# The local attention's result: transposed by VectorE on its way to DRAM, or by TensorE on its way back

## The chip, the core and the metric

One core of a Trainium2 chip. Its engines are TensorE (PE, with PEld for its weight loads), VectorE (DVE), ScalarE (ACT), GpSimd (POOL) and SyncE (SP), which issues nearly all the DMAs. The metric is the device time of one execution in microseconds, the median of several runs.

## The reference

Two attentions over the same input x (2048 positions, 448 features, 16 heads of 28), mixed by a gate. All is float32.

```python
x = A_x
g = sigmoid((x * gate_w).sum(-1, keepdims=True))
# A, local: position s looks at s, s-2, ..., s-14 (eight places)
logits = einsum("bhsd,bhswd->bhsw", q, k[s - 2w]) * 28 ** -0.5   # masked where s - 2w < 0
a = (softmax(logits) applied to v[s - 2w]).reshape(B, S, D) @ A_wo
# B, full: softmax(q k^T * 28 ** -0.5) v over all 2048 positions
b = (...).reshape(B, S, D) @ B_wo
return g * a + (1 - g) * b
```

## The kernel before, in words

Each float32 operand of a matmul is split into two parts, a rounded one (`hi`) and the rest (`lo`), and a product is three matmuls (hi hi, hi lo, lo hi; `TERMS`). The program is written for five engines in an order of its own; nothing is reordered afterwards, and each engine works through its list in order.

**First stage** (to about 260 us): the projections of x to q, k, v of both attentions.

**Attention, 256 steps.** A unit `u` (0 to 15) is four heads and 512 queries; a step is one block of 128 keys of a unit (`kt`, sixteen in a unit), so step 121 is unit 7, block 9. In a step PE makes the scores of the four heads (function `scores`, L1024), ACT takes two exponentials (L1027, each of 128x1024, into one of the tiles `P`), and PE multiplies the step before's probabilities with V (`do_av`, L978). In the trace a step begins with its first exponential. The maxima that the softmax of B needs are made ahead: in steps 0 to 234 PE also makes up to three plain score tiles (L144) and DVE reduces them (L148, a tile of 128x512 and then a pair); the pair's bank serves the next step's scores.

**Local attention beside it.** Attention A runs on POOL and DVE during those steps, in eight chunks of two heads. A chunk `c` is: eight products q k (POOL, `a_score`, L613) with their sums (DVE, `a_reduce`, L623), a softmax (`a_softmax`), and eight products with v and seven adds into the tile `oat` (POOL, `a_av`, L663 and L668). Rows of `oat` are positions (128 partitions x 16), columns 2 heads of 28. A planner writes the order: `item(engine, key, name, cost, needs, f)` puts an instruction on an engine's list, `needs` are names with a lag in steps, and `issue` takes at each step, in order of key, what is due. It books the costs of POOL and DVE against about 2.25 us a step; POOL may be booked up to 4.2 us behind, DVE up to 0.7. Four steps after a chunk's last add one DMA puts `oat` into `oa_scr` in DRAM, by positions.

**Output projection.** When the planner's lists are empty (`a_done`, step 217) the output weights are loaded and split (`raw_wo`, `split_wo`). From step 236 on, `op_some` puts items of a queue (`op_queue`) behind each step, seven a step: for each of sixteen blocks `j` of 128 positions, the local result is loaded (`op_load_a`), transposed by PE (`op_t`, four transposes, L795), split by ACT and DVE (`op_split`, L803 to L806) and multiplied (`op_mm`, L817) with the weights, together with B's result, which is feature-major already (`op_load_b`, from `on_hi` and `on_lo`). Blocks 12 to 15 and the rest of 8 to 11 come after the last step. Working tiles come from a ring of eight buffers of 128x512 (`mtile`).

B's result of a unit goes through a chain of its own, one unit later (`fin_copy` to `fin_store`): the sum of the exponentials to DRAM and back, its inverse spread, a product on POOL, a split, a store.

## Time and profile before

| | |
|---|---|
| median of 3 runs | 918.61 us (916.68 to 918.8) |
| the profiled execution | 918.6 us, its span 916.7 us |
| granted TensorE clock | 0.997 |
| busy | PE 904.7, DVE 731.4, ACT 652.1, POOL 620.9 us |
| 300 to 700 us | POOL busy 43.7 to 49.6 of every 50 us, DVE 47.2 to 49.2 |
| 800 to 880 us | POOL busy 0 to 1.3 of every 20 us, DVE 1.5 to 2.2, PE 20.0 |

The profile is of one execution. A group's line tells the code line, the engine, the operation, the tiles (out<-in), shapes and count, then the busy time in us, the mean duration of one in ns, and the idle time of the engine ahead of it with what ended it. A line of the timeline begins with its start and length in us. PE's matmuls are pipelined: the next one starts before the last one's end, so that the distance of starts tells what one costs, not its duration.

### The profile page before, as it was taken

The page shows a single profiled execution, that of the slowest core. Times are in us where ns is not written, and L with a number is a line of the kernel's source. Part 1 is how long each engine was busy: PE and PEld are TensorE (multiplying, and loading weights), DVE is VectorE, ACT ScalarE, POOL GpSimd, SP SyncE. Part 2 cuts the span into 40 slices and gives each one's busy share as a digit, 9 for nine tenths or more (in the row PEclk, how much of TensorE's full clock was granted, in tenths as well). Part 3 has the DMA queues.
Part 4 walks back from the last instruction along what each step waited for, and adds up shares of the span by engine and source line. Part 5 has one row for each costly group of instructions (what it writes and reads, how often), then busy time and mean ns, then how long its engine had stood idle before and what let it go on. Part 6 is the DMA issues. An engine that isn't in the chain of part 4 may idle for free.

```text
span 916.7 us, 20680 instructions
## 1 busy us (share of the span) xinstructions
PE 904.7 (99%) x8396; PEld 539.3 (59%) x8396; DVE 731.4 (80%) x977; ACT 652.1 (71%) x802; POOL 620.9 (68%) x485
## 2 busy tenths in 40 slices
PE   9899999999999999999999999999999999999998
PEld 7688999999954444444444444443444444466667
DVE  6388999999979999999999999999999888400012
ACT  6356434343378898888888898988989889854551
POOL 2289856564469799999999999999994952300100
PEclk9999999999999999999999999999999999999999
DMA  9867603444372341335135232530412123553422
GB/s 268 275 203 220 177 11 83 132 122 120 103 249 70 97 126 44 86 112 127 44 96 153 86 102 55 144 79 23 115 42 53 34 66 102 145 162 112 131 90 93
DMA packets 101118, 104.29 MB, mean 114 GB/s; under 512 B 61652, under 2 KB 71252, under 8 KB 100240
## 3 DMA queue, kind: packets, MB, share of 16 engines
q1 hardware_dynamic: 100880, 102.72, 39.5%
q8 instruction: 65, 1.06, 0.5%
q10 hardware_dynamic: 144, 0.26, 0.1%
q14 instruction: 29, 0.24, 0.1%
HBM read 61.99 MB, written 40.48 MB: 112 GB/s over the span
## 4 chain that ended last, share of the span: by engine, by line
PE 80%; POOL 11%; DMA 3%; SPq 2%; ACT 2%; issue 1%; DVE 0%; POOLq 0%; ACTq 0%; DVEq 0%
PE T L1024 22%; PE av L978 20%; PE r L298 15%; PE T L817 8%; PE r L293 7%; PE r L144 4%; POOL prod L613 3%; POOL oat L668 3%; PE T L144 3%; POOL prod L663 2%; SPq L101 2%; ACT P L1027 1%; PE T L795 1%; DMA KL<-qk_lo 1%; DMA V<-in_xT 1%
## 5 line engine op out<-in xcount | busy, mean ns | idle before, releaser
L1027 ACT ACTIVATE P<-T 128x1024 f32<-128x1024 f32 x512 | 497.4, 1025 | 81.0 <-PE T L1024 79.6
L148 DVE TENSOR_REDUCE MX<-T 128x1 f32<-128x512 f32 x470 | 441.3, 954 | 33.6 <-PE T L144 19.6
L978 PE MATMUL av<-P,V 128*32 128x512 f32 x2048 | 272.7, 605 | 0.0
L1024 PEld LDWEIGHTS T<-QH,KH 30*128 30x128 f32 x1024 | 90.8, 181 | 222.4 <-ACT P L1027 199.9
L144 PE MATMUL T<-KH,QP 28*128 28x512 f32 x704 | 219.6, 454 | 0.1
L162 DVE TENSOR_REDUCE MX<-r 128x2 f32<-128x1024 f32 x160 | 192.5, 1221 | 28.3 <-PE r L144 23.6
L1024 PE MATMUL T<-QH,KH 30*128 30x512 f32 x1024 | 211.2, 489 | 3.0 <-ACT P L1027 2.0
L1024 PE MATMUL T<-QH,KL 28*128 28x512 f32 x1024 | 185.7, 395 | 0.0
L1024 PE MATMUL T<-QL,KH 28*128 28x512 f32 x1024 | 183.5, 392 | 0.0
L613 POOL TENSOR_TENSOR prod<-qt,kt 128x896 f32<-128x896 f32 x64 | 135.2, 2117 | 1.4 <-DMA kt<-a_scr 1.4
L362 ACT ACTIVATE raw<-r 128x896 f32<-128x896 f32 (+1 forms) x64 | 58.9, 921 | 96.7 <-PE r L298 96.7
L668 POOL TENSOR_TENSOR oat<-oat,prod 128x896 f32<-128x896 f32 x56 | 118.3, 2113 | 2.4
L144 PE MATMUL r<-KH,QP 64*128 64x512 f32 x320 | 98.9, 393 | 3.4 <-DMA KH<-qk_hi 3.4
L144 PEld LDWEIGHTS T<-KH,QP 28*128 28x128 f32 x704 | 86.0, 181 | 27.1 <-ACT P L1027 20.3
L663 POOL TENSOR_TENSOR prod<-vt,L 128x896 f32<-128x896 f32 x56 | 95.6, 1708 | 0.5
L363 POOL TENSOR_TENSOR ast<-raw 128x448 f32<-128x448 f32 x48 | 55.5, 1156 | 57.8 <-ACT raw L362 49.4
L1024 PEld LDWEIGHTS T<-QL,KH 28*128 28x128 f32 x1024 | 93.3, 184 | 0.0
L1024 PEld LDWEIGHTS T<-QH,KL 28*128 28x128 f32 x1024 | 91.8, 183 | 0.9
L298 PE MATMUL r<-wh,xh 64*128 64x448 f32 (+1 forms) x512 | 87.8, 363 | 0.0
L978 PEld LDWEIGHTS av<-P,V 128*32 128x32 f32 x2048 | 40.3, 108 | 77.2 <-issue 72.2
L805 DVE TENSOR_TENSOR oalo<-T,oah 128x384 fp32r<-128x384 f32 x16 | 8.9, 557 | 90.8 <-ACT onhi L804 87.7
L298 PE MATMUL r<-wh,xl 64*128 64x448 f32 (+1 forms) x384 | 70.9, 363 | 0.0
(110 smaller groups left out, 1157.0 us busy)
## 6 DMA issues: line engine op xcount, KB each, us to landing
a_scr<-ast SPq DMA_DIRECT2D x24, 448.0 KB
qk_hi<-qkh SPq DMA_DIRECT2D x24, 256.0 KB
qk_lo<-qkh SPq DMA_DIRECT2D x24, 256.0 KB
rbc<-rs SPq DMA_DIRECT2D x60, 64.0 KB
QP<-qk_hi SPq DMA_DIRECT2D x64, 56.0 KB
KL<-qk_lo SPq DMA_DIRECT2D x16, 224.0 KB
QH<-qk_hi SPq DMA_DIRECT2D x64, 56.0 KB
QL<-qk_lo SPq DMA_DIRECT2D x64, 56.0 KB
```

The lines of the kernel that those rows point to most:

```text
L144: nc.tensor.matmul(bank, qhis[u][h % 2][r, 128 * qs:128 * qs + 128], KH[u // NB % 3][r, 512 * kc:512 * kc + 512], start=True, stop=True)
L148: r = nc.vector.tensor_reduce(MX[:, n % NMX:n % NMX + k], bank, axis=X, op=ALU.max)
L162: nc.vector.tensor_reduce(m, PM[k], axis=X, op=ALU.max)
L293: nc.tensor.matmul(bank, ws[c][rows, k, t[4]:t[4] + 128], x, start=first, stop=last)
L298: nc.tensor.matmul(bank[:, 0:cols], x, ws[c][rows, k, 0:cols], start=first, stop=last)
L613: nc.gpsimd.tensor_tensor(out=p, in0=qt[c], in1=kvt["k", c % 2][:, HALO - DIL * w:HALO - DIL * w + NJ, :], op=ALU.mult)
L663: nc.gpsimd.tensor_tensor(out=dst.rearrange("p j (h d) -> p j h d", d=DH), in0=kvt["v", c % 2][:, HALO - DIL * w:HALO - DIL * w + NJ, :].r ...
L668: nc.gpsimd.tensor_tensor(out=oat[c], in0=oat[c], in1=oat[c, w], op=ALU.add)
L817: writes(bank, nc.tensor.matmul(bank[:, :D], src, wo[c][:, k, :], start=(first and k == ks[0] and i == 0), stop=(last and k == ks[-1] and ...
L978: nc.tensor.matmul(av[32 * h:32 * h + 32, :], V[:, kt, 4 * g + h, :], tiles_[h], start=(kt == 0), stop=(kt == NJ - 1), skip_group_check=True)
L1024: nc.tensor.matmul(bank[a], (KH[g % 3], KH[g % 3], KL[g % 2])[t][r, ks], (qh, ql, qh)[t][r, :], start=(t == 0), stop=(t == 2))
L1027: e = nc.scalar.activation(p, RP[0] if a == "2" else mine, AF.Exp, scale=SCALE).ins
```

## The change

`oat` gets rows of 32 for each head (28 used, the rest zero): two tiles `oats` that alternate. After a chunk's last add DVE transposes it in 32x32 blocks, four instructions of 128x256 (`a_turn`, new line L676), and eight DMAs (`a_store`, two for each group of 32 partitions) write the blocks' rows, 32 values of 4 bytes a piece, into `oa_scr`, which is now feature-major. Both are items of the planner. The projection then loads four tiles of 512 positions for each of four blocks `b`, and DVE and POOL split them (`op_split`, into parts of the old K tiles, `spare`, that the attention no longer reads). `op_t` is gone from PE. The projection queue is served five items a step instead of seven. There are four tiles `P` instead of eight.

```diff
-    oa_scr = dram.tile([128, NJ, D], F32, name="oa_scr")
+    oa_scr = dram.tile([D, S], F32, name="oa_scr")
-    probs = [ep.tile([128, 2, 512], F32, name=f"P{i}") for i in range(8)]
+    probs = [ep.tile([128, 2, 512], F32, name=f"P{i}") for i in range(4)]
+    oats = [a1.tile([128, NJ, 2, 32], F32, name=f"oat{i}") for i in range(2)]
+    for t in oats:
+        nc.gpsimd.memset(t, 0.0)
...
-            if w == W - 1:
-                stored[0] = now[0] + 4
-                at("end", stored[0], lambda: nc.sync.dma_start(oa_scr[:, :, 56 * c:56 * c + 56], oat[c]))
+    def a_turn(c, i):
+        if i == 0:
+            oaTt[c] = a2.tile([128, NJ, 2, 32], F32, name="oatT")
+        r = slice(4 * i, 4 * i + 4)
+        nc.vector.transpose(oaTt[c][:, r].rearrange("p j h e -> p (j h e)"),
+                            oats[c % 2][:, r].rearrange("p j h e -> p (j h e)"))
+    def a_store(c, a):
+        for h in range(2):
+            f = 56 * c + DH * h
+            nc.sync.dma_start(oa_scr[f:f + DH].rearrange("f (j p) -> f j p", j=NJ)[:, :, 32 * a:32 * a + 32],
+                              oaTt[c][32 * a:32 * a + DH, :, h, :])
...
+        for i in range(4):
+            item("dve", c0 + 53 + i, ("t", c, i), 0.35, [(("a", c, W - 1, 1), 1), (("t", c, i - 1), 0)],
+                 lambda c=c, i=i: a_turn(c, i))
+            item("sp", c0 + 59 + i, ("st", c, i), 0, [(("t", c, 3), 2), (("st", c, i - 1), 1)],
+                 lambda c=c, i=i: a_store(c, i))
...
+    def op_load_a(b):
+        cs = slice(512 * b, 512 * b + 512)
+        for k in range(4):
+            raws[b, k] = mtile("oar")
+            n = 128 if k < 3 else 64
+            nc.sync.dma_start(raws[b, k][0:n, :], oa_scr[128 * k:128 * k + n, cs])
+    def op_split(b, k):
...
+        nc.vector.tensor_copy(hi, raw)
+        nc.gpsimd.tensor_tensor(out=lo, in0=raw, in1=hi.bitcast(F32), op=ALU.subtract)
-    def op_t(j):
...
-            (0, lambda: op_t(j + 1)),
-            (0, lambda: op_split(j + 1)),
...
-    at("end", OP0 + 3, lambda: (op_load_a(0), op_load_a(1)))
+    at("end", OP0 + 3, lambda: op_load_a(0))
+    for k in range(4):
+        at("dve", OP0 + 6 + k, lambda k=k: op_split(0, k))
...
-                op_some(st, 7)
+                op_some(st, 5)
```

The first place is DVE in steps 120 to 122, where chunk 3's last add has been issued to POOL in step 120. A step's rows are the two maxima (L148) and what the planner adds behind them; L623 and L626 are the same sums of the local scores. Before:

```order
L623 TENSOR_REDUCE L<-prod 128x16 x2
L148 TENSOR_REDUCE MX<-T_3283 128x1
L148 TENSOR_REDUCE MX<-T_3271 128x2
L148 TENSOR_REDUCE MX<-T_3283 128x1
L148 TENSOR_REDUCE MX<-T_3275 128x2
L623 TENSOR_REDUCE L<-prod 128x8 x2
```

And in the changed kernel:

```order
L626 TENSOR_REDUCE L<-prod 128x16 x2
L148 TENSOR_REDUCE MX<-T_3283 128x1
L148 TENSOR_REDUCE MX<-T_3271 128x2
L676 STREAM_TRANSPOSE oatT<-oat_3316 128x256
L148 TENSOR_REDUCE MX<-T_3283 128x1
L148 TENSOR_REDUCE MX<-T_3275 128x2
L626 TENSOR_REDUCE L<-prod 128x8 x2
```

The first of the chunk's four transposes stands in the step right behind the add's, ahead of the next step's maxima.

The second place is PE in the first step with projection work, step 236. `oah` and `oalo` are the split local result, `KH` (in the changed kernel) the old K tiles that hold it, `onhi` and `onlo` B's result with the local result's last 64 features. Before:

```order
L817 MATMUL T_3271<-wo_9729,oah 128x448
L817 MATMUL T_3271<-wo_9730,oah 128x448
L817 MATMUL T_3271<-wo_9729,oalo 128x448
L795 MATMUL T_3283<-ident,oal 128x128 x3
L795 MATMUL T_3283<-ident,oal 64x128
L817 MATMUL T_3271<-wo_9729,oah 128x448
L817 MATMUL T_3271<-wo_9730,oah 128x448
L817 MATMUL T_3271<-wo_9729,oalo 128x448
L1024 MATMUL T_3279<-QH,KH_151 128x512 x2
```

After (L831 is L817, L1036 is L1024):

```order
L831 MATMUL T_3271<-wo_9946,KH_3289 128x448
L831 MATMUL T_3271<-wo_9947,KH_3289 128x448
L831 MATMUL T_3271<-wo_9946,KH_3289 128x448
L831 MATMUL T_3271<-wo_9946,onhi_10238 128x448
L831 MATMUL T_3271<-wo_9947,onhi_10238 128x448
L831 MATMUL T_3271<-wo_9946,onlo_10239 128x448
L831 MATMUL T_3271<-wo_9946,onhi_10240 128x448
L831 MATMUL T_3271<-wo_9947,onhi_10240 128x448
L831 MATMUL T_3271<-wo_9946,onlo_10241 128x448
L1036 MATMUL T_3279<-QH,KH_151 128x512 x2
```

The transposes are gone, and the step's projection work is fifteen matmuls where it was nine and a set of transposes.

The third place is PE at the end of step 255, where the projection's queue has run out in the changed kernel. L978 and L990 are the products with V; L862 and L876 begin the last unit's own chain. Before:

```order
L817 MATMUL T_3271<-wo_9729,onhi_10630 128x448
L817 MATMUL T_3271<-wo_9730,onhi_10630 128x448
L817 MATMUL T_3271<-wo_9729,onlo_10631 128x448
L978 MATMUL av<-P_3301,V 32x512
L978 MATMUL av<-P_3300,V 32x512 x2
L978 MATMUL av<-P_3301,V 32x512
L817 MATMUL T_3271<-wo_9729,onhi_10632 128x448
```

After:

```order
L990 MATMUL av<-P_3295,V 32x512
L990 MATMUL av<-P_3294,V 32x512 x2
L990 MATMUL av<-P_3295,V 32x512
L990 MATMUL av<-P_3297,V 32x512
L990 MATMUL av<-P_3296,V 32x512 x2
L990 MATMUL av<-P_3297,V 32x512
L831 MATMUL T_3271<-wo_9946,onhi_10660 128x448
```

Step 254's products with V are followed at once by step 255's; the twelve projection matmuls that stood between them stand in earlier steps.

More of the change, by code (lines that the diff above doesn't have):

```diff
@@ L789, in op_load_b @@
             dma_r(t[p0:p0 + n], src[r0:r0 + n, 512 * b:512 * b + 512])
-    def op_t(j):
-        t = oaT[j]
-        for k in range(4):
-            n = 128 if k < 3 else 64
-            writes(side["t"], nc.tensor.transpose(side["t"][0:n, 128 * k:128 * k + 128], t[:, 128 * k:128 * k + n], ident))
-    def op_split(j):
-        b, jj = divmod(j, 4)
-        bank = side["t"]
-        cs = slice(128 * jj, 128 * jj + 128)
-        hi, lo = mtile("oah").bitcast(F32R), mtile("oalo").bitcast(F32R)
-        th, tl = on_tiles(b)[0]
-        nc.scalar.activation(hi[:, :384], bank[:, :384], AF.Copy)
-        nc.scalar.activation(th[0:64, cs], bank[0:64, 384:512], AF.Copy)
-        nc.vector.tensor_tensor(out=lo[:, :384], in0=bank[:, :384], in1=hi[:, :384].bitcast(F32), op=ALU.subtract)
-        nc.vector.tensor_tensor(out=tl[0:64, cs], in0=bank[0:64, 384:512], in1=th[0:64, cs].bitcast(F32),
-                                op=ALU.subtract)
-        oaT[j] = (hi, lo)
     TERMS = ((0, 0), (0, 1), (1, 0))
@@ L928, in s1_close @@
         accs.extend(sums(1 - turn[0]))
-        side["f"], side["t"] = accs[1], T1
+        side["f"] = accs[1]
         order.extend([*pbank[0], *sums(turn[0])])
@@ L1025, in scores @@
             if t == 2 and a in "20":
-                p = probs[len(exps) % 8]
+                p = probs[len(exps) % 4]
                 e = nc.scalar.activation(p, RP[0] if a == "2" else mine, AF.Exp, scale=SCALE).ins
-                if len(exps) >= 8:
-                    tc.declare_no_dep(e, exps[-8], reason="the matmuls that read it came between")
+                if len(exps) >= 4:
+                    tc.declare_no_dep(e, exps[-4], reason="the matmuls that read it came between")
                 exps.append(e)
@@ L1046, in op_some @@
                 opj[0] += 1
+                b, i = divmod(j, 4)
+                if i == 0:
+                    op_load_a(b + 1)
+                    if b:
+                        for k in range(3):
+                            op_load_b(b + 1, k)
+                elif i == 2:
+                    for k in range(4):
+                        op_split(b + 1, k)
             if opq[0][0] > st:
@@ L1055, in gated_mix_kernel @@
             st = NJ * u + kt
-            now[0] = st
             if kt == 12 and u + 1 < NU:
@@ L1062, in gated_mix_kernel @@
                 issue("pool", st, 4.2)
-            if not adone and not any(lists.values()) and st > stored[0]:
+            if not adone and not any(lists.values()):
                 a_done(st)
```

38 lines of the change are left out of this document (16 added, 22 removed).

## The prediction

> **What bounds the kernel now.** I read the page first (busy shares, then the chain that ended last), then the table of stretches, then the groups by line and shape, and last the timeline at the places that the change touches.
>
> ```profile
> span 916.7 us, 20680 instructions
> PE 904.7 (99%) x8396; PEld 539.3 (59%) x8396; DVE 731.4 (80%) x977; ACT 652.1 (71%) x802; POOL 620.9 (68%) x485
> PE 80%; POOL 11%; DMA 3%; SPq 2%; ACT 2%; issue 1%; DVE 0%; POOLq 0%; ACTq 0%; DVEq 0%
> ...
> 450.00:500.00 50.00, 50.00 (x511) 20.75 (x506) 48.57 (x75) 44.23 (x50) 49.14 (x34) 1.00 0.40 107
> 840.00:860.00 20.00, 20.00 (x142) 13.07 (x142) 2.24 (x6) 11.06 (x17) 1.29 (x1) 1.00 0.20 60
> ```
>
> The last two lines are stretches; their columns are PE, PEld, DVE, ACT, POOL, then granted clock, DMA share, GB/s. PE is never idle in either, but only the second belongs to PE alone. From about 260 to 790 us (the attention steps with the running maxima, 2.25 us each) DVE is about 97% and POOL 98% busy beside PE. From 795 us on (the output projection) DVE and POOL stand still and only PE counts. The change takes work from PE in the second stretch and gives work to DVE in the first, so the two have to be priced apart.
>
> **What PE saves.** The 64 transposes of the local result (L795) go.
>
> ```profile
> L795 PE MATMUL T<-ident,oal 128*128 128x128 f32 x48 | 7.9, 274 | 0.0
> L795 PE MATMUL T<-ident,oal 128*64 128x128 f32 x16 | 4.4, 273 | 0.0
> 790.39 0.65 PE L795 MATMUL T<-ident,oal 128*128 128x128 f32 x4
> 790.98 0.51 PE L1024 MATMUL T<-QH,KH 30*128 30x512 f32 x4
> ...
> 902.61 0.60 PE L795 MATMUL T<-ident,oal 128*128 128x128 f32 x4
> 902.97 0.65 PE L817 MATMUL T<-wo,oah 128*128 128x448 f32 x2
> ```
>
> By duration that is 12.3 us, but the durations overlap. What counts is the time from a set's start to the next matmul's start: 0.59 us for the first of the sixteen sets, 0.36 for the last, 6.8 in all (the same difference summed over all sixteen). The matmul behind a set is also about 0.09 us late (0.29 to the next one where 0.20 is usual), in ten of the sixteen: 0.9. Five sets end a step; without them the change from projection to scores still costs its 0.1: minus 0.5. That leaves 7.2. The first set lies in a step without projection work, where PE will then wait for ACT instead (next row group): minus 0.3. PE saves 6.9 us.
>
> [...] The starts in the rows are 0.11 us apart, so I take 6.8; the other value is a rival below.
>
> **What the end of the attention loses.** Counted in the program's order, the projection queue shrinks from 140 items to 92, but is now served five a step instead of seven. It runs dry in the last step but one, which gets two items, and the last step gets none. What a step without projection costs, the trace shows once, before the projection starts:
>
> ```profile
> 791.99 1.94 ACT L1027 ACTIVATE P<-T 128x1024 f32<-128x1024 f32 x2 [0.75 <-PE T L1024]
> 793.07 0.50 PE L1024 MATMUL T<-QH,KH 30*128 30x512 f32 x2
> 793.98 0.50 PE L1024 MATMUL T<-QH,KH 30*128 30x512 f32 x2 [0.41 <-ACT P L1027]
> ...
> 886.23 1.07 PE L978 MATMUL av<-P,V 128*32 128x512 f32 x8
> 886.34 1.94 ACT L1027 ACTIVATE P<-T 128x1024 f32<-128x1024 f32 x2 [2.01 <-PE T L1024]
> 889.89 1.06 PE L978 MATMUL av<-P,V 128*32 128x512 f32 x8
> ```
>
> The second half of the scores waits 0.9 us for the exponential. At the end, the last products (889.89) come 3.66 us behind the ones before them, with 2.7 us of projection between. Without it they follow at 887.2 and wait for the second exponential, done at 888.3: 1.1 us. The scores of the last step lose 0.9 less the 0.7 of one projection item ahead of them: 0.2. Together 1.3 us. So the projection and the end gain 6.9 - 1.3 = 5.6 us.
>
> **What DVE pays.** 32 transposes of 128x256 come in.
>
> ```profile
> L186 DVE STREAM_TRANSPOSE nms<-nmt 128x32 f32<-128x32 f32 x16 | 3.2, 202 | 1.1 <-POOL nmt L181 1.1
> L623 DVE TENSOR_REDUCE L<-prod 128x16 f32<-128x224 f32 x80 | 28.4, 373 | 0.0
> L148 DVE TENSOR_REDUCE MX<-T 128x2 f32<-128x1024 f32 x234 | 286.1, 1223 | 8.7 <-PE T L1024 1.9 <-PE T L144 0.5
> L148 DVE TENSOR_REDUCE MX<-T 128x1 f32<-128x512 f32 x236 | 162.4, 688 | 24.8 <-PE T L144 19.1 <-PE T L1024 3.3
> ```
>
> The two L148 rows give 1.045 ns an element (535 ns for 512 more). At that slope a transpose of 256 takes 202 + 224 x 1.045 = 436 ns. If each 32x32 block had to fill and drain apart, the 202 ns would split into about 135 fixed and 67 a block, and eight blocks would take 670. I take 0.44, by the slope of the maxima, the nearest rows that show one; 0.67 stays for the range. [...]
>
> 32 x 0.44 = 14 us on an engine that is idle about 1.4 of 50 us. They are not put on blindly: the planner that fills DVE's steps books 0.35 for each and pushes reductions back, so that the local attention ends five steps later (222 instead of 217) with the projection still starting at step 236. In a step with one reduction and one transpose the pair takes about 0.07 us more than two reductions (0.67) do; some eight such steps, and four with two transposes (0.15 each), make 1.2 us if PE feels each. It can feel them:
>
> ```profile
> 505.89 1.81 DVE L148 TENSOR_REDUCE MX<-T 128x1 f32<-128x512 f32 x2
> 507.76 0.18 PEld L1024 LDWEIGHTS T<-QH,KH 30*128 30x128 f32 x2 [0.22 <-DVE MX L148]
> ```
>
> The maxima end at 507.70, and the scores that reuse their bank start at 507.76. DVE has no time in hand there.
>
> **The wait that the transposes bring.** This is the largest term. A chunk's transposes need POOL's last add (L668), and the planner lets them follow one step behind it, while it lets POOL run up to 4.2 us behind its plan. In the new order chunks 3, 4, 6 and 7 have their first transpose in the very next step; 0, 1, 2 and 5 three to seven steps later. Chunk 3's add keeps its step, so the trace of before shows what its transpose will meet:
>
> ```profile
> 532.83 1.81 DVE L148 TENSOR_REDUCE MX<-T 128x1 f32<-128x512 f32 x2
> 533.14 1.94 ACT L1027 ACTIVATE P<-T 128x1024 f32<-128x1024 f32 x2 [0.34 <-PE T L1024]
> 534.05 2.12 POOL L668 TENSOR_TENSOR oat<-oat,prod 128x896 f32<-128x896 f32 x1
> 534.87 2.03 DVE L148 TENSOR_REDUCE MX<-T 128x1 f32<-128x512 f32 x2 [0.23 <-PE T L144]
> ...
> 741.65 1.94 ACT L1027 ACTIVATE P<-T 128x1024 f32<-128x1024 f32 x2 [0.36 <-PE T L1024]
> 742.00 2.11 POOL L668 TENSOR_TENSOR oat<-oat,prod 128x896 f32<-128x896 f32 x1
> 743.35 2.06 DVE L148 TENSOR_REDUCE MX<-T 128x1 f32<-128x512 f32 x2
> ```
>
> DVE is done with the maxima of the step at 534.64 and would start the transpose; the add ends at 536.17. The transpose then ends at 536.6, and the next maxima start there instead of at 534.87. They may start 0.3 us later than that at no cost (after two reductions they start 0.31 us ahead of their step's exponential, 532.83 against 533.14, and PE does not wait), so PE loses about 1.4 us. Behind the transpose on DVE stand those maxima; for them PE's scores wait, and no later step gives the time back, since the step is PE's own 2.25. Chunk 7 alike: its add ends at 744.11, 2.46 us into the step after it was issued, and its two transposes end near 744.9, where 743.6 would be free: 1.2 us. Chunk 4's add moves two steps ahead, to where the planner books POOL 1.6 us further behind: 1.2 us, a little less than its 1.4 since POOL has caught up some of the first stall. Chunk 6's is issued with little booked: 0.4. Together 4.2 us, from 0 (if POOL is there in time) to about 6.
>
> **The rest, at nothing.** POOL's 56 adds and 8 first products now write rows of 28 in 32. The nearest rows lie on both sides:
>
> ```profile
> L668 POOL TENSOR_TENSOR oat<-oat,prod 128x896 f32<-128x896 f32 x56 | 118.3, 2113 | 2.4
> L618 POOL TENSOR_TENSOR prod<-prod 128x448 f32<-128x448 f32 x40 | 41.0, 1026 | 3.1
> L363 POOL TENSOR_TENSOR V<-raw 128x448 f32<-128x448 f32 x16 | 18.4, 1155 | 12.5 <-ACT raw L362 12.5
> L761 POOL TENSOR_TENSOR wo<-wor,wo 128x448 fp32r<-128x448 f32 x7 | 8.0, 1147 | 14.0 <-ACT wo L760 14.0
> L412 DVE CAST xh<-V 128x512 fp32r<-128x512 f32 x2 | 0.9, 471 | 4.6 <-DMA V<-in_xT 4.6
> L885 POOL TENSOR_TENSOR on<-osb,rbc 128x512 f32<-128x512 f32 x15 | 19.3, 1290 | 25.6 <-DMA rbc<-rs 18.2 <-DMA QH<-qk_hi 7.3
> L671 SPq DMA_DIRECT2D oa_scr<-oat x8: 573/580/607, 370.7 to 751.4; - x8
> ```
>
> L363 writes just such rows (28 of 32) in 1155 ns, as long as the contiguous 448 of L761: no change, and I take that. L618, in place over rows of 14 in 28, is 11% shorter (1026): an add of 1.88, a gain of 0.23. Upward, L761's 2.56 ns an element would make 2.29, 0.18 more. Both ends go into the rivals. The two clears of the padded tiles stand on POOL ahead of the first loads. The splits move from ACT and DVE (32 and 32 instructions) to DVE and POOL (16 casts of 0.47, 16 subtractions of at most 1.29) into the stretch where those two are idle; their cover is the projection itself, since a block's four loads and splits are issued while PE works on the block before. SP gets 64 stores for 8; at most the 0.58 us of L671 each, two a step, behind which loads stand that are needed four steps later. The first raw loads share a ring of eight buffers with the raw output weights and wait for two of their splits, about one step; the splits stand three to six steps behind: nothing, up to 2 us if I misjudge. Four probability tiles instead of eight: the products that read a tile stand on PE ahead of the scores whose exponential rewrites it, so no new wait.
>
> **Sum.** The profiled execution took 918.6 us (span 916.7 and 1.9 around it), as the median of the runs, 918.6. Minus 5.6, plus 4.2, plus a third of the 1.2 (0.4; most steps have a little in hand): 918.6 - 1.0, rounded against the unknown 2 us of the loads to 917.5 us. One case measured against another must differ by 0.3% (2.8 us) here to be told from no change.
>
> **The rivals.**
> - The likeliest, 0.40: as summed, 917.5, its own range 915 to 919.5.
> - POOL is in time, 0.33: the strided add is as short as L618 suggests. Seven adds a chunk, 1.7 us earlier at its end, cover the 1.2 to 1.4 of chunks 3, 4 and 7. Then the gain of PE stays: 918.6 - 5.6 + 0.4 = 913.4. The same comes if PE's earlier delays let POOL catch up. For it speaks L618; against it L363.
> - PE saves the transposes by their full duration, 0.02: 12.3 instead of 6.8 makes 917.5 - 5.5 = 912.0; the starts 0.11 us apart speak against it. [...]
> - The padded add is longer, 0.12, the side on which it is slower: POOL is busy 49.14 of 50 us where the chunks run, so from about 1 us in 50 (0.1 us an add) its delay reaches every chunk's reductions, not only the transposes. At 0.18 an add, 10 us of POOL, of which I put 6 on PE: 923.5. Against it L363.
> - The transpose takes 0.67, 0.08: 32 x 0.23 = 7.4 us more on DVE, nearly all felt as the row at 507.76 shows: 917.5 + 5 = 922.5.
> - The change leaves the time as it was, since the projection waits for its late loads: 0.05, 918 to 919.
>
> Faster by over 0.3%: the second and third, and a twentieth of the first's tail, 0.39. Slower by over 0.3%: 0.20. Within: 0.41. The range, 911.5 to 922.5, leaves out the worse half of the two slower cases and the lower tail of the second.
>
> **What would show it.** Right: no L795 rows on PE; PE from the start of the projection to the end shorter by 5 to 7 us; a gap of about 1 us ahead of the last products; the new transposes at 0.40 to 0.47 us; DVE waiting for POOL's add one to two us in chunks 3, 4 and 7, and in the same places steps of 3.4 us. Wrong: adds off 2.11 us by over 0.1; transposes near 0.67; mean steps before the projection above 2.30 without such waits; PE waiting for casts or raw loads at the projection's start.

## The result, and the profile after

| | before | after |
|---|---|---|
| median of the runs | 918.70 us (916.68 to 919.47) | 925.33 us (922.72 to 926.46) |
| profiled execution | 918.6 us, span 916.7 | 922.72 us, span 920.9 |

The ratio is 1.0066, 95% interval 1.0042 to 1.0089: slower by 0.66%, where 917.5 us was forecast and the range ended at 922.5. The profiled execution of after is the shortest of its six, 2.6 us under their median, so the tables below show less than the whole difference. One execution on record, the profiled one of e8 below, took 3934 us; it is of no use here, so e8 has no trace.

The page of after, first its span and PE's row, then the chain that ended last, then the two stretches that the prediction began with (PE, PEld, DVE, ACT, POOL, granted clock, DMA share, GB/s):

```profile
span 920.9 us, 20595 instructions
PE 904.2 (98%) x8332; PEld 533.7 (58%) x8332; DVE 739.9 (80%) x993; ACT 643.1 (70%) x770; POOL 643.3 (70%) x503
...
PE 71%; POOL 17%; DMA 5%; SPq 2%; DVE 2%; issue 2%; ACT 1%; POOLq 0%; ACTq 0%; DVEq 0%
...
450.00:500.00 50.00, 48.44 (x486) 20.07 (x483) 46.60 (x75) 42.02 (x48) 49.05 (x34) 0.97 0.39 104
840.00:860.00 20.00, 20.00 (x139) 13.04 (x138) 3.74 (x5) 9.34 (x12) 7.02 (x6) 1.00 0.43 129
```

PE's busy time hardly falls (904.7 to 904.2 us) though 64 matmuls are gone, and in the attention stretch it now stands still for 1.6 of 50 us, at a granted clock of 0.97. In the chain, PE fell from 80% to 71%, POOL rose from 11 to 17, DMA from 3 to 5. What PE stands still for, the table of waits says, before (first row) and after (second):

```profile
PE T L1024 <- DMA QH<-nm: 0.7, 1, 0.7
...
PE T L1036 <- DMA QH<-nm: 4.7, 2, 3.2
```

These are the query loads of two units (us in total, times, longest). The groups that the prediction priced, in after:

```profile
L676 DVE STREAM_TRANSPOSE oatT<-oat 128x256 f32<-128x256 f32 x32 | 13.3, 426 | 1.2 <-POOL oat L670 1.2
L186 DVE STREAM_TRANSPOSE nms<-nmt 128x32 f32<-128x32 f32 x16 | 3.2, 203 | 3.6 <-POOL nmt L181 3.6
L670 POOL TENSOR_TENSOR oat<-oat,prod 128x896 f32<-128x896 f32 x56 | 118.1, 2110 | 2.4
L595 POOL MEMSET oat<- 128x1024 f32 x2 | 1.8, 944 | 0.0
L682 SPq DMA_DIRECT2D oa_scr<-oatT x64: 785/795/1070, 396.3 to 772.3; - x64
```

The transpose takes 426 ns (436 forecast) and POOL's padded add 2110 (2113 before): two terms right to 3%. The last row is the one that matters: a store occupies SP's queue for 0.795 us in the median, where the prediction had "at most the 0.58 us of L671".

Where the time went is told by the steps. A step begins with its first exponential (L1027 before, L1039 after); the table gives, for each stretch of steps, the time over that of the same stretch in the trace of before, in us. Step 0 begins at about 260 us; what lies ahead of it is the same code in every kernel and differs from run to run, so it has a column of its own.

| kernel | to step 0 | 0-15 | 16-79 | 80-111 | 112-127 | 128-159 | 160-207 | 208-223 | 224-235 | 236-end |
|---|---|---|---|---|---|---|---|---|---|---|
| after | +0.9 | +0.8 | -0.7 | +2.9 | +0.1 | +3.5 | +0.4 | +1.2 | +0.3 | -5.3 |
| e1: stores late | +1.5 | +1.6 | -0.7 | +0.3 | +3.4 | 0.0 | +0.4 | +1.2 | +0.1 | -5.3 |
| e2: before with stores | +0.7 | 0.0 | -0.6 | +1.4 | 0.0 | +5.4 | 0.0 | 0.0 | 0.0 | 0.0 |
| e3: no transposes | +0.3 | +0.8 | -0.8 | +3.2 | -0.1 | +5.7 | +0.1 | 0.0 | +0.3 | -5.3 |
| e4: lag 3 | -0.2 | +0.8 | -0.8 | +3.6 | 0.0 | +6.6 | +0.2 | +0.1 | +0.3 | -5.3 |
| e5: late, lag 3 | -2.0 | +0.8 | -0.8 | +0.4 | +0.2 | -0.3 | +0.2 | +0.1 | +0.3 | -5.3 |
| e6: and paced | +0.9 | +0.8 | -0.7 | +0.3 | +0.2 | -0.3 | +0.2 | +0.1 | +0.3 | -6.4 |
| e7: clears on DVE | +0.9 | +0.9 | -0.7 | +0.4 | +0.1 | +0.2 | +0.2 | +0.1 | +0.3 | -6.6 |
| e9: row stores | +1.7 | +1.5 | -0.8 | +0.4 | +3.2 | +2.8 | +0.3 | +1.2 | +0.2 | -5.2 |
| e10: rows, lag 3, paced | +0.1 | +0.8 | -0.7 | +0.3 | +0.1 | +7.4 | +0.1 | +0.1 | +0.3 | -6.6 |
| e11: key load later | +1.2 | +0.8 | -0.8 | +3.9 | +0.1 | 0.0 | +0.4 | +1.2 | +0.2 | -5.3 |
| e12: all remedies | +1.0 | +0.8 | -0.9 | +0.4 | +0.1 | -0.3 | +0.2 | +0.1 | +0.3 | -6.6 |

Two stalls stand in the trace of before alone and count as a gain in every other row, not as one of the change: 0.7 us in step 79 (in the column 16-79), and 1.2 us in step 158 (3.51 us against 2.35 everywhere else, in the column 128-159), where PE waits 1.07 us for an exponential that stands on ACT behind an instruction waiting for POOL. And e1 and e9 have 0.7 to 0.8 us more than the others in 0-15, from a stretch of half clock in step 1 (see the last section).

In after, the end gains 5.3 and steps 80 to 111 and 128 to 159 lose 6.4. The losses are steps 94 to 97 (2.51, 3.54, 3.20 and 2.59 us) and steps 143 and 144 (5.33 and 3.47), where the other steps of these stretches stay near 2.25 (143 and 144 together are 4.4 us longer than before's; the column's 3.5 has the 1.2 of step 158 taken off): the ends of units 5 and 8, where the next unit's queries come in. The second place on SP's queue, in the timeline (start, time, line, number of issues), before and then after:

```profile
568.34 0.34 SPq L851 DMA_DIRECT2D rs<-finv  x1
568.78 1.65 SPq L101 DMA_DIRECT2D KL<-qk_lo  x4
...
575.64 1.61 SPq L101 DMA_DIRECT2D QH<-qk_hi  x4
577.29 3.07 SPq L101 DMA_DIRECT2D QL<-qk_lo  x4
580.40 1.05 SPq L101 DMA_DIRECT2D QH<-nm  x2
```

```profile
571.16 0.35 SPq L865 DMA_DIRECT2D rs<-finv  x1
571.56 3.61 SPq L682 DMA_DIRECT2D oa_scr<-oatT  x4
575.27 1.81 SPq L101 DMA_DIRECT2D KL<-qk_lo  x4
...
578.92 1.99 SPq L682 DMA_DIRECT2D oa_scr<-oatT  x2
...
583.35 1.70 SPq L101 DMA_DIRECT2D QH<-qk_hi  x4
585.09 3.50 SPq L101 DMA_DIRECT2D QL<-qk_lo  x4
588.64 1.11 SPq L101 DMA_DIRECT2D QH<-nm  x2
```

SP's issues go out one behind the other: in these rows none starts before the one ahead of it has ended (571.16 and 0.35, then 571.56; 585.09 and 3.50, then 588.64). Until 568.34 (571.16) SP waits for POOL's `finv` (8.2 and 5.0 us); everything that the planner put into the steps of that wait then goes out at once. From there to the last query load (`QH<-nm`) it took 12.1 us before and 17.5 after, 5.4 more, which is the six stores (5.6); little is left for their traffic on the DMA engines. PE, at the same place:

```profile
583.92 0.50 PE L1024 MATMUL T<-QH,KH 30*128 30x512 f32 x2
```

```profile
587.07 1.07 PE L990 MATMUL av<-P,V 128*32 128x512 f32 x8
591.32 0.50 PE L1036 MATMUL T<-QH,KH 30*128 30x512 f32 x2 [3.18 <-DMA QH<-nm]
592.44 1.72 PE L990 MATMUL av<-P,V 128*32 128x512 f32 x8
594.09 0.79 PE L1036 MATMUL T<-QH,KH 30*128 30x512 f32 x2
```

After, PE goes on 2.7 us behind the start of the `nm` issues (591.32 against 588.64). Before, those issues stood 3.5 us ahead of their use (580.40, 583.92): 0.8 us in hand. The `finv` comes 1.3 us earlier within its step than before (571.16 against a step 143 at 586.98; before 568.34 against 582.84). So 5.4 - 1.3 - 0.8 = 3.3 us late, and the row says 3.18.

The last two rows show a second cost: the products with V take 1.72 us where they took 1.07, a pair of scores 0.79 where it took 0.50. The windows there, one us each, say why (the last figures are granted clock, DMA share, GB/s):

```profile
592.00:593.00 1.00, 1.00 (x15) 0.24 (x12) 1.00 (x2) 0.69 (x1) 1.00 (x1) 0.86 0.00 0
593.00:594.00 1.00, 1.00 (x8) 0.00 (x0) 1.00 (x2) 1.00 (x2) 1.00 (x2) 0.50 0.00 0
594.00:595.00 1.00, 1.00 (x12) 0.83 (x12) 0.10 (x2) 0.85 (x2) 1.00 (x1) 0.50 0.00 0
595.00:596.00 1.00, 1.00 (x11) 0.36 (x7) 0.65 (x1) 0.22 (x1) 1.00 (x3) 0.50 0.00 0
596.00:597.00 1.00, 1.00 (x11) 0.16 (x8) 0.79 (x1) 1.00 (x2) 1.00 (x1) 0.93 0.59 93
```

The clock is halved for 3.4 us, which loses 1.7 us (0.14 + 3 x 0.50 + 0.07) on top of the wait.

### The profile page after: what moved, and what is told of

Same layout as the page of the kernel before. It is cut to its first block, busy times and chain, and to the rows that moved or that the text cites. A ratio compares the mean times of both kernels' runs of the same rounds, so it can differ in the third digit from the quotient of the medians.

```text
span 920.9 us, 20595 instructions
## 1 busy us (share of the span) xinstructions
PE 904.2 (98%) x8332; PEld 533.7 (58%) x8332; DVE 739.9 (80%) x993; ACT 643.1 (70%) x770; POOL 643.3 (70%) x503
## 4 chain that ended last, share of the span: by engine, by line
PE 71%; POOL 17%; DMA 5%; SPq 2%; DVE 2%; issue 2%; ACT 1%; POOLq 0%; ACTq 0%; DVEq 0%
PE T L1036 18%; PE av L990 16%; PE r L298 15%; PE T L831 8%; PE r L293 7%; POOL oat L670 5%; POOL prod L665 5%; PE r L144 4%; POOL prod L616 4%; PE T L144 2%; DMA KL<-qk_lo 1%; DVE MX L148 1%; DMA kt<-a_scr 1%; SPq L101 1%; POOL prod L621 1%
## 5 line engine op out<-in xcount | busy, mean ns | idle before, releaser
L1039 ACT ACTIVATE P<-T 128x1024 f32<-128x1024 f32 x512 | 497.0, 1024 | 104.7 <-PE T L1036 103.4
L148 DVE TENSOR_REDUCE MX<-T 128x1 f32<-128x512 f32 x470 | 439.0, 952 | 30.9 <-PE T L144 16.8
L990 PE MATMUL av<-P,V 128*32 128x512 f32 x2048 | 274.0, 607 | 0.8 <-ACT P L1039 0.8
L1036 PEld LDWEIGHTS T<-QH,KH 30*128 30x128 f32 x1024 | 91.5, 182 | 231.0 <-ACT P L1039 200.8
L1036 PE MATMUL T<-QH,KH 30*128 30x512 f32 x1024 | 213.7, 491 | 7.2 <-DMA QH<-nm 4.7
L1036 PE MATMUL T<-QH,KL 28*128 28x512 f32 x1024 | 186.7, 397 | 0.0
L1036 PE MATMUL T<-QL,KH 28*128 28x512 f32 x1024 | 184.8, 395 | 0.0
L616 POOL TENSOR_TENSOR prod<-qt,kt 128x896 f32<-128x896 f32 x64 | 134.9, 2113 | 0.2
L670 POOL TENSOR_TENSOR oat<-oat,prod 128x896 f32<-128x896 f32 x56 | 118.1, 2110 | 2.4
L1036 PEld LDWEIGHTS T<-QL,KH 28*128 28x128 f32 x1024 | 94.3, 186 | 0.0
L1036 PEld LDWEIGHTS T<-QH,KL 28*128 28x128 f32 x1024 | 92.9, 184 | 1.2
L990 PEld LDWEIGHTS av<-P,V 128*32 128x32 f32 x2048 | 40.3, 108 | 81.4 <-issue 75.1
L298 PE MATMUL r<-wl,xh 64*128 64x448 f32 (+1 forms) x448 | 68.2, 367 | 0.0
```

The lines of the kernel that those rows point to most:

```text
L148: r = nc.vector.tensor_reduce(MX[:, n % NMX:n % NMX + k], bank, axis=X, op=ALU.max)
L298: nc.tensor.matmul(bank[:, 0:cols], x, ws[c][rows, k, 0:cols], start=first, stop=last)
L616: nc.gpsimd.tensor_tensor(out=p, in0=qt[c], in1=kvt["k", c % 2][:, HALO - DIL * w:HALO - DIL * w + NJ, :], op=ALU.mult)
L670: nc.gpsimd.tensor_tensor(out=oat[c], in0=oat[c], in1=oat[c, w], op=ALU.add)
L990: nc.tensor.matmul(av[32 * h:32 * h + 32, :], V[:, kt, 4 * g + h, :], tiles_[h], start=(kt == 0), stop=(kt == NJ - 1), skip_group_check=True)
L1036: nc.tensor.matmul(bank[a], (KH[g % 3], KH[g % 3], KL[g % 2])[t][r, ks], (qh, ql, qh)[t][r, :], start=(t == 0), stop=(t == 2))
```

## The experiments

Medians are compared with runs of the kernel before on the same chip: 918.34 us beside e1 to e4, 919.39 beside e5 to e8, 919.09 beside e9 and e10, 919.14 beside e11 and e12. The theory: the stores delay the query loads on SP, and the wait of DVE for POOL that the prediction named is there too, but hidden. The rival: the transposes, or the order into which they push the reductions, cost the time.

**e1: the stores late.** The planner lets a chunk's stores onto SP only in the last four steps of a unit, where they come behind the next unit's query loads.

```diff
-            if any(d in names and issued.get(d, 10 ** 6) + lag > st for d, lag in needs):
+            if any(d in names and issued.get(d, 10 ** 6) + lag > st for d, lag in needs) or (
+                    name[0] == "st" and st % NJ < 12):
```

> The changed kernel with one thing moved: the stores of the transposed result are issued only in blocks 12 to 15 of a unit, behind the next unit's query loads, instead of as soon as they are due. Same instructions on every engine. Theory SP (eight stores of 0.8 us each stand on SP, behind its wait for POOL's finv and ahead of the query loads, so units 6 and 9 start late): the long steps at 95 to 97 (+2.9 us) and 143 to 144 (+4.6) go; 925.3 becomes 917 to 918.5. Theory order (the planner's shifted reductions and transposes on DVE and POOL cost the time): 925 stays.

Measured: 919.30 us, ratio 1.0008 (0.9992 to 1.0024), 6.0 us under after's median and 0.8 over the expected range, which left out what now appears. The waits for QH are gone, with steps 94 to 97 and 143 to 144. In their place stand new long steps: 122 and 123 (4.22 and 3.80), 146 (3.11), 216 (3.29). The first of them, in the timeline of e1:

```profile
537.31 2.12 POOL L670 TENSOR_TENSOR oat<-oat,prod 128x896 f32<-128x896 f32 x1
539.47 0.45 DVE L676 STREAM_TRANSPOSE oatT<-oat 128x256 f32<-128x256 f32 x1 [2.11 <-DMA vt<-a_scr]
...
540.54 0.50 PE L144 MATMUL T<-KH,QP 28*128 28x512 f32 x1 [0.73 <-DVE MX L148]
541.67 0.50 PE L1037 MATMUL T<-QH,KH 30*128 30x512 f32 x2 [0.63 <-DVE MX L148]
542.58 1.83 PE L991 MATMUL av<-P,V 128*32 128x512 f32 x8
```

DVE stands idle for 2.11 us ahead of chunk 3's first transpose. The row blames a load, but POOL's last add ends at 539.43, 0.04 us ahead of the transpose. That is the prediction's wait, at its place. PE then waits twice (0.73 and 0.63) for the maxima behind it, and runs at half clock after that (1.83 for 1.07 us; granted 0.50 from 543 to 546 us). So the stores had hidden it: while PE stood still for queries, POOL caught up. (e9 below agrees: where the stall at unit 6 goes, steps 122 and 123 are long again, 4.03 and 3.81; where that at unit 9 stays, step 146 is not.)

**e2: the kernel before, with 56 stores.** Stores of nearly the same form (pieces of 112 bytes for 128), from the untransposed result to a place that nothing reads, in the steps where after has those of chunks 0 to 6.

```diff
+            nc.sync.dma_start(dm_scr[f:f + DH].rearrange("f (j p) -> f j p", j=NJ)[:, :, 32 * a:32 * a + DH],
+                              oat[c][32 * a:32 * a + DH, :, DH * h:DH * h + DH])
+    for c, st in enumerate((60, 85, 110, 134, 159, 186, 198)):
+        for i in range(4):
+            at("pre", st + i, lambda c=c, i=i: dummy(c, i))
```

> The kernel before, with 56 stores added: eight for each of the first seven chunks, from the local result's tile to a spare DRAM tensor that nobody reads, of the form of the changed kernel's stores (28 partitions, 16 runs of 112 bytes, to rows 8 KB apart) and at the steps where the changed kernel has them. DVE, POOL, PE and ACT keep the order of before. Theory SP: the late queries of units 6 and 9 appear here too, 918.7 becomes 924 to 927. Theory order: 918 to 920.

Measured: 926.22 us, ratio 1.0091 (1.0072 to 1.0110): 7.9 us for the stores alone. The wait and the issue:

```profile
PE T L1035 <- DMA QH<-nm: 6.0, 2, 4.6
...
L679 SPq DMA_DIRECT2D dm_scr<-oat x56: 787/795/1212, 395.1 to 723.5; - x56
```

In the table all of it lies in steps 80 to 111 and 128 to 159; the other stretches stay at nothing, but for the 0.6 us that every kernel gains in 16 to 79.

**e3: no transposes.** All else is kept; the stores send the untransposed tiles, so that the kernel leaves out the local part of the result as such.

```diff
-        nc.vector.transpose(oaTt[c][:, r].rearrange("p j h e -> p (j h e)"),
-                            oats[c % 2][:, r].rearrange("p j h e -> p (j h e)"))
+        oaTt[c] = oats[c % 2]
```

> The changed kernel without the 32 transposes on DVE: the stores read the untransposed padded tiles, so the local attention's part of the output is left out as such. The planner still books the transposes, so that all else keeps its step. Theory SP: only the wait of chunk 7 for POOL (1.2 us) and the transposes' own share go, 923.5 to 925. Theory DVE (32 transposes of 0.43 us and their waits for POOL are what slows the steps): 917 to 920.

Measured: 923.11 us, ratio 1.0053 (1.0036 to 1.0070). That is 0.4 under the expected range. Both long places stay (+3.2 and +5.7), and of the wait for POOL chunk 7's goes (208 to 223: 0.0 for +1.2). The rival falls.

**e4: lag 3.** The transposes become due three steps behind POOL's last add.

```diff
-            item("dve", c0 + 53 + i, ("t", c, i), 0.35, [(("a", c, W - 1, 1), 1), (("t", c, i - 1), 0)],
+            item("dve", c0 + 53 + i, ("t", c, i), 0.35, [(("a", c, W - 1, 1), 3), (("t", c, i - 1), 0)],
```

> The changed kernel with the transposes due three steps behind POOL's last add instead of one. My predicted term (DVE waiting for POOL in chunks 3, 4 and 7) said 4 us; the profile after shows it in chunk 7 alone, 0.9 us. Theory SP: 923.5 to 925, the waits of units 6 and 9 for their queries stay unless the stores happen to move past them. The predicted term: 921.

Measured: 924.90 us, ratio 1.0075 (1.0055 to 1.0095). Chunk 7's wait goes, and the wait for QH grows from 4.7 to 7.3 us. Alone, this remedy is worth nothing that can be told from no change.

**e5: both remedies**, the edits of e1 and e4 together.

> The changed kernel with both remedies: a chunk's stores are let onto SP only in the last four steps of a unit, behind the next unit's query loads, and the transposes become due three steps behind POOL's last add instead of one. Theory (two queues, one hides the other: the stores delay the query loads, and where they don't, DVE waits for POOL's add): with late stores alone the profile showed the waits for POOL in steps 122 and 123 (3.5 us over 2.25 together), 146 (0.9) and 216 (1.0); all three go, so 919.3 - 5.4 = 913.9, between 912.5 and 915.5, with no step between 4 and 232 above 2.5 us. Rival (POOL is the bound over the chunks, so a transpose that no longer waits leaves the delay to the next reduction): DVE or PE waits for POOL elsewhere in the same chunks, 917 to 919.5.

Measured: 915.78 us, ratio 0.9957 (0.9942 to 0.9972), no wait for QH and none of DVE for POOL's last add. The median lies 0.3 us over the expected interval, on a chip whose runs of before are 1 us longer than those beside e1; in steps 80 to 223 the two profiles show +5.4 for e1 and +0.6 for e5, 4.8 us for the waits, where the prediction had 4.2.

**e6: paced.** The 92 projection items are served 5, 5, 5, 4, 4 a step, so that the last two steps have four each instead of two and none.

```diff
-                op_some(st, 5)
+                op_some(st, 5 if (st - OPS[0]) % 5 < 3 else 4)
```

> As the kernel with late stores and transposes three steps behind, but the 92 projection items are served 5, 5, 5, 4, 4 a step instead of five, so that the last two attention steps have four each instead of two and none. The prediction put 1.3 us on the empty last step (the last products wait 1.1 us for the exponential, its scores 0.2). Theory: that comes back, 912.6 if the other kernel takes 913.9, and no wait ahead of the last products. Rival (the last step's items only take the place of the wait, and steps of four items wait for the exponential themselves): within 0.4 us of the other kernel.

Measured: 913.94 us, ratio 0.9943 (0.9926 to 0.9960). The end gains 6.4 us in place of 5.3, so the empty last step cost 1.1; the products no longer wait for the exponential. The medians differ by 1.8, more than the trace shows, with overlapping runs.

**e7: the clears elsewhere.** As e6, with the clears of the padded tiles on DVE in steps 4 and 5.

```diff
-    for t in oats:
-        nc.gpsimd.memset(t, 0.0)
+    for i in range(2):
+        at("dve", 4 + i, lambda i=i: nc.vector.memset(oats[i], 0.0))
```

> As the paced kernel, but the two clears of the padded tiles go from POOL, where they stand ahead of the negated maxima and the key clear (L595, 1.83 us for both), to DVE in steps 4 and 5. Theory: step 3 waits 1.2 us on DVE for POOL's negated maxima because of the clears, 0.8 us of it felt; that goes, so 0.8 us below the paced kernel, about 911.8. Rival: POOL's own chain (the clear of KH and the first products) is late anyway, no change; or the clears on DVE delay the maxima of steps 4 and 5 by their length, and the gain is given back.

Measured: 914.45 us, ratio 0.9956 (0.9942 to 0.9970), no gain. Step 3 is no longer long (3.03 us in e6), but steps 5 and 6 are (2.53 and 2.75): steps 0 to 15 cost +0.9 where e6 has +0.8. The rival was right: the two clears cost about the same ahead of DVE's maxima on either engine. This trace also has a wait of 1.0 us for QH at unit 9, with no store ahead of the query loads: there, SP waits 1.5 us until PE has read the key buffer and 2.4 us for the chunk's `kt` loads (0.4 and 1.7 in e6, where PE does not wait for QH). So the place stays tight without the stores too.

**e8: four tiles of probabilities** in the kernel before, and nothing else (`range(8)` to `range(4)`, `% 8` to `% 4`, `exps[-8]` to `exps[-4]`).

> The kernel before with four tiles of probabilities instead of eight, and nothing else. Theory: the products that read a tile stand on PE ahead of the scores whose exponential rewrites it, so no wait arises: the time of before, 918.3, within 1 us. Rival: ACT waits for a free tile where PE is late (the stalls of steps 79 and 158 would be longer), 919.5 to 921.

Measured: 919.28 us, ratio 1.0010 (0.9996 to 1.0024): nothing, as forecast.

**e9: row stores.** Is it the number of the stores or their form? The padded tile keeps the two heads apart, so that a store is 28 rows of 2 KB in place of 448 pieces of 128 bytes. The places stay.

```diff
-    oats = [a1.tile([128, NJ, 2, 32], F32, name=f"oat{i}") for i in range(2)]
+    oats = [a1.tile([128, 2, NJ, 32], F32, name=f"oat{i}") for i in range(2)]
...
-            nc.sync.dma_start(oa_scr[f:f + DH].rearrange("f (j p) -> f j p", j=NJ)[:, :, 32 * a:32 * a + 32],
-                              oaTt[c][32 * a:32 * a + DH, :, h, :])
+            nc.sync.dma_start(oa_scr[f:f + DH, a], oaTt[c][32 * a:32 * a + DH, h].rearrange("p j e -> p (j e)"))
```

> The changed kernel with the same 64 stores at the same places, but each of 28 rows of 2 KB in place of 448 pieces of 128 bytes (the padded tiles keep the two heads apart, and the four reads of a block take rows of 512 bytes). This asks whether the number of the stores or their form costs SP's time. Theory (form): an issue falls from 0.82 us to that of the plain row transfers, 0.34 to 0.43 us; the six stores ahead of unit 9's query loads then take 2.4 instead of 5.6 us, the wait of PE for QH falls from 4.7 us to under 1, steps 143 and 144 to under 3 us; the waits of DVE for POOL's add then show in chunks 3, 4 and 7 as with late stores: 918 to 920. Rival (number: an issue costs 0.8 us whatever its form): as the changed kernel, 924 to 926.

Measured: 921.92 us, ratio 1.0035 (1.0020 to 1.0050): between the two theories.

```profile
L682 SPq DMA_DIRECT2D oa_scr<-oatT x64: 307/384/1852, 397.7 to 771.2; - x64
...
PE T L1035 <- DMA QH<-nm: 2.3, 1, 2.3
```

The form halves the issue, 0.795 to 0.384 us, as the first theory had it, and the stall at unit 6 goes (80 to 111: +0.4). That at unit 9 shrinks only from 3.2 to 2.3 us. The expectation of under 1 us there was wrong: what stands ahead of these query loads is more than the stores. SP also waits, in this run, for a key buffer to be read and for a chunk's loads to land:

```profile
SPq L864 <- POOL finv L860: 6.0, 1, 6.0
SPq L101 <- DMA kt<-a_scr: 3.3, 2, 2.3
SPq L101 <- PE T L144: 1.9, 2, 1.6
```

The second row comes of a rule of the compiled program, seen in its order of SP's instructions (here five rows of after): the transfers take eight semaphores in turn, DMAHW0 to 7, and each waits until the transfer eight places ahead has landed. (In the trace of after the 873 issues of SP take the eight in turn throughout; the store at 571.56 and the `rbc` load at 577.13, eight places on, wait for and raise the same one.)

```
L101 DMA QL_5078<-qk_lo_60 28x512 [waits DMAHW1_49]
L101 DMA QL_5078<-qk_lo_60 28x512 [waits DMAHW2_49]
L101 DMA QL_5078<-qk_lo_60 28x512 [waits DMAHW3_49]
L101 DMA QL_5078<-qk_lo_60 28x512 [waits DMAHW4_49]
L101 DMA QH_5073<-nm4_104 4x512 [waits DMAHW5_49]
```

In e9 the last two `QL` issues wait 2.3 and 1.0 us for the two `kt` loads eight places ahead of them, and no store stands between. The same two waits are there in before (0.6 and 1.0) and in after (0.6 and 1.4), so they are not the stores' own. How the 2.3 us of PE divide between these waits, the key buffer's (1.9) and the stores' issues was not measured apart.

**e10: row stores, lag 3, paced**, without holding the stores back.

> Row stores as above at the planner's own places (not held back to the end of a unit), transposes three steps behind POOL's last add, and the projection items paced 5, 5, 5, 4, 4. Theory (form): as the paced kernel with late stores, 913 to 915, without a wait for QH. Rival (the stores ahead of the query loads still delay them, 2 to 3 us in steps 95 and 143): 916 to 919.

Measured: 920.92 us, ratio 1.0011 (0.9997 to 1.0026): beyond the rival's 919 too, a miss. The one wait for QH is the longest of all, 6.8 us at unit 9 (step 143: 9.24). With lag 3 a store's transpose comes later, and SP waits 1.8 us for one, in order, ahead of the queries.

**e11: the key load later.** As after; only the reload of a key buffer that step 192 needs moves from step 136 to 148, behind unit 9's query loads.

```diff
-                          (100, 3, KH[0], qk_hi), (136, 3, KL[1], qk_lo)):
+                          (100, 3, KH[0], qk_hi), (148, 3, KL[1], qk_lo)):
```

> The changed kernel, where only the reload of KL's second buffer (four transfers of 224 KB, needed at step 192) moves from the end of step 136 to the end of step 148, behind unit 9's query loads. It asks what else the query loads stand behind. Theory (the stores used up a slack that was small because the key reload and a chunk's loads stand ahead of the same query loads): the four issues (1.8 us) and the wait for their landing go from ahead of unit 9's query loads, so the wait of 3.2 us in step 143 shrinks to under 0.5, steps 143 and 144 lose about 3.5 of their 4.3 us over 2.25; chunk 4's wait for POOL may show (0.9): 921 to 922.5. Steps 95 to 97 stay as they are. Rival (the stores' own time is what is late): the stall shrinks by less than 2 us, 923.5 to 925.5.

Measured: 920.19 us, ratio 1.0003 (0.9987 to 1.0019). That is 0.8 under the expected range. Step 143 falls from 5.33 to 3.23 us, step 144 from 3.47 to 2.30, steps 128 to 159 from +3.5 to 0.0. The wait at unit 9 falls from 3.2 to 1.1 us, and not to under 0.5 as expected. The other wait, at unit 6, which the edit does not touch, is 2.2 here and was 1.6 in after (80 to 111: +3.9 for +2.9). The stores are still 0.796 us each. So the stores did not act alone: they used up a slack that was small because a key reload, a chunk's loads and the `finv` wait stand ahead of the same queries.

**e12: all remedies**: e9's form, e1's place, e4's lag, e6's pace.

> All remedies: row stores, held back to the last four steps of a unit behind its query loads, transposes three steps behind POOL's last add, projection items paced 5, 5, 5, 4, 4. Theory: no wait for QH and none for POOL; 913 to 914.5, as the paced kernel with the stores in pieces, since behind the query loads their length no longer counts. Rival (the longer stores still delay a next unit's first transfers in steps 126 and 142, which were 0.4 to 0.6 us long): 0.5 to 1 us below the paced kernel.

Measured: 913.42 us, ratio 0.9930 (0.9908 to 0.9952): faster than before by 0.7% and than after by about 12 us, though not to be told from e6. Its chain that ended last is PE's again, 94% where before had 80:

```profile
PE 94%; DMA 2%; DVE 1%; SPq 1%; ACT 1%; POOL 0%; issue 0%; ACTq 0%; DVEq 0%; POOLq 0%
```

## Why the prediction was wrong

**The step that failed is in "The rest, at nothing":** "SP gets 64 stores for 8; at most the 0.58 us of L671 each, two a step, behind which loads stand that are needed four steps later." Each part of it fails. A store took 0.795 us: it has 448 pieces where L671 has 2048 (128 partitions of 16), and yet it took longer. They do not go out two a step: SP waits for `finv` (5.0 us in after at this place, 8.2 before), and what the planner booked in those steps follows in one row. And what stands behind them could not wait four steps: at unit 9 it had 0.8 us in hand. e2 prices this step by itself at 7.9 us.

The trace of before had the sign of it. Its table of waits has PE waiting 0.7 us for QH, once, at 438.81. SP's rows ahead of that show the same order, a store among it:

```profile
421.97 0.34 SPq L851 DMA_DIRECT2D rs<-finv  x1
...
428.05 0.60 SPq L671 DMA_DIRECT2D oa_scr<-oat  x1
429.84 4.01 SPq L101 DMA_DIRECT2D QH<-qk_hi  x4
...
436.96 1.07 SPq L101 DMA_DIRECT2D QH<-nm  x2
```

The store's own 0.60 us is the smaller part of that lateness: two of the query issues behind it took 2.73 and 1.74 us where 0.38 is usual, while the DMA share was 1.00 to 1.30 in each us from 428 to 434. But a queue that is late once is worth measuring at its other places of the same kind; at unit 9 the same distance gives 0.8 us in hand, against six stores. (That wait did not recur: all later kernels, e2 included, are 0.6 to 0.9 us shorter in steps 16 to 79.)

**The wait that the transposes bring, 4.2 us: there, but hidden, and near the forecast in its sum by luck.** In after only chunk 7's shows:

```profile
754.43 2.10 POOL L670 TENSOR_TENSOR oat<-oat,prod 128x896 f32<-128x896 f32 x1
...
756.57 0.77 DVE L676 STREAM_TRANSPOSE oatT<-oat 128x256 f32<-128x256 f32 x2 [0.94 <-POOL oat L670]
757.26 1.78 DVE L148 TENSOR_REDUCE MX<-T 128x1 f32<-128x512 f32 x2
```

Two transposes directly behind the add, and a step of 3.31 us: 1.1 over, 1.2 forecast. With the stores out of the way (e1 less e5) the four chunks cost 4.8. Chunk 3 was undersized: 3.2 us (112 to 127) for 1.4, of which 1.7 is the halved clock that the prediction did not have. Chunk 4 was oversized, 0.3 (128 to 159) for 1.2, and chunk 6 too, 0.2 (160 to 207) for 0.4; chunk 7 is 1.1 (208 to 223) for 1.2. The two errors nearly cancel.

**What PE saves, and the end.** 5.3 us from step 236 on, 5.6 forecast. Without the empty step 6.4 to 6.6 (e6, e12), 6.9 forecast; the empty step 1.1, 1.3 forecast. The products at the end of after wait as the prediction said, 0.81 us for the exponential:

```profile
893.24 1.94 ACT L1039 ACTIVATE P<-T 128x1024 f32<-128x1024 f32 x2 [0.41 <-PE T L1036]
895.24 1.06 PE L990 MATMUL av<-P,V 128*32 128x512 f32 x8 [0.81 <-ACT P L1039]
```

The transposes went by their starts (0.11 us apart in before's row at 902.61), not by their durations (273 and 274 ns): the rival of 12.3 us falls.

**What DVE pays.** 0.426 us each for 0.436, against the 0.67 of the rival. Felt by PE, with the waits removed, at most 0.6 us (e5, steps 80 to 223), 0.4 forecast. The 0.67 came of a split of the 202 ns into 135 fixed and 67 a block, which was the author's supposition; no run shows it. The slope between the two transposes of 256 and 32 elements, (426 - 203) / 224 = 1.0 ns an element, is near that of the maxima (1.045).

**The rest of "the rest".** The padded add is unchanged (2110 ns), so both rivals built on it fall. The clears cost 0.8 us (steps 0 to 15), not nothing: their 1.83 us on POOL stand ahead of the negated maxima that the L186 transposes wait for, 3.6 us in all in the row above, 1.1 before. The late raw loads of the projection did not come. Four tiles cost nothing (e8).

Put together, with the measured sizes the sum without the SP step is 918.6 - 5.3 + 4.8 + 0.6 + 0.8 = 919.5. That is well inside the range, and e1, which is that kernel, took 919.3; it is no separate test, since 4.8 and 0.6 are read from the traces of e1 and e5. So the range failed by the SP step, the term that was put at nothing and given no range upward. The forecast of 917.5 would have been about 2 us low without it: the clears (0.8), the wait (0.6), PE's saving (0.3), DVE (0.2). One thing stays open: the profile of after, from step 0 on, accounts for 3.2 us over before, while its median is 6.6 over. Its other five executions have no trace. In e3, which has the same stores in the same steps, steps 128 to 159 cost 5.7 us for after's 3.5, so the stall may vary from run to run by some us; e3 lacks the transposes, so this is not shown.

## To carry to other kernels

Price an added DMA on the queue that issues it: its issue time, from a row of the same form if there is one (a smaller transfer may take longer: here 56 KB took 0.795 us, 448 KB 0.580), and then the time in hand of the first load behind it whose data an engine waits for, read as the distance from that load's issue to its first use at every place where it recurs, the worst one counting. A wait of even 0.7 us on that load in the profile before says that there is none in hand at that place, and that the other places are to be read too. When one wait hides another, remedies have to be tried together: late stores alone and late transposes alone gave 0.1% over before and 0.75% over, both together 0.4% under.

## What the runs showed of the hardware

**Some short idle times of PE were followed by half the clock.** This is from the traces of before, after, e1 to e7 and e9 to e12, from step 0 to 900 us. Single idle times of PE of 1.56 and 3.18 us (after) and of 2.20 (e11) were each followed by 3.4 us at a granted clock of 0.50, which loses 1.7 us. With those of 1.79 (e3) and 2.08 us (e4), in steps 80 to 111, and 2.26 (e9), in steps 128 to 159, the table's columns are 1.4, 1.5 and 1.7 us longer than the idle time alone (the 1.2 of step 158 added back in the second column). With 4.58 (e2), 4.66 (e3), 5.20 (e4) and 6.80 us (e10), all in steps 128 to 159, they are 2.0, 2.2, 2.6 and 1.8 us longer; in e10 the clock was low before the idle time ended (0.55 from 588 to 592 us, where PE goes on at 591.53). Two idle times close together were followed by the half clock too: 0.73 and 0.63 in e1 (0.50 from 543 to 546 us, 3.4 us in all); 0.56 and 0.64 in e9 go with +3.2 us in steps 112 to 127, where e1 has +3.4. Other single ones of 0.45 to 1.46 us lost nothing (in before, those of 0.7 us in step 79 and 1.07 us in step 158 stand at a granted clock of 1.00), but for one: an idle time of 0.52 us in step 0, the same in all these traces, was followed by the half clock in e1 and e9 alone (0.50 from 264 to 266 us). So the length alone does not decide, and what else does these rows don't tell. With the wait of 1.56 us, after's steps 94 to 97 took 2.8 us longer than before's.

**A store's issue time went with its form, not with its bytes.** At the same 56 KB, 448 pieces of 128 bytes occupied SP's queue for 0.795 us (after), 28 rows of 2 KB for 0.384 (e9). The number of pieces is not all: L671 (before) has 2048 pieces of 224 bytes, 448 KB, and took 0.580. What sets the time beyond that was not varied.
